# One instruction order for all engines, a narrower chunk mask and a crossbar transpose for two more pairs of heads, in an attention and feed-forward kernel

## The chip, the cores and the metric

The kernel runs on one core of a Trainium2 chip. The metric is the device time of one execution in microseconds (us), lower is better; the time before is the median of three runs. A core has five engines that each work through their own list of instructions: TensorE (PE in the profile, with its weight loads as PEld), VectorE (DVE), ScalarE (ACT), GpSimd (POOL), and SyncE (SP), which here only issues transfers. They wait for each other through semaphores. Sixteen DMA engines move data.

## The reference

The first half is causal attention over four batches of eight heads, 768 positions, head dimension 64. The keys are divided into 24 chunks of 32; each query keeps the six chunks with the highest upper bound on its score. The second half is a feed-forward block with a spatial gate.

```
k_min, k_max = min, max of k over each chunk of 32
ub     = sum_d max(q * k_min, q * k_max)             # a bound for each query and chunk
ub     = where(chunk is not later than the query's own, ub, -1e9)
top    = argsort(ub)[-6:]
scores = q @ k.T / 8, kept where the key's chunk is in top and key <= query
attn   = softmax(scores) @ v                         # -> x, (4, 768, 512)

h    = relu(x @ w_in);  u, v = h[:512], h[512:]      # per token
v_n  = (v - mean(v)) / sqrt(var(v) + 1e-6)
v_s  = w_spatial @ v_n + b_spatial                   # across the tokens
out  = (u * v_s) @ w_out
```

## The kernel before

The 32 heads are worked in 16 pairs, four pairs to a batch. A pair is first prepared: the keys are transposed on TensorE, VectorE takes the maximum and minimum of each chunk, the queries are transposed and split into a positive and a negative part, and matmuls of 48 columns (two heads of 24 chunks) form the bounds. A mask matmul opens the group and pushes later chunks down. VectorE then takes the best eight and marks the chunks below the sixth.

```python
def bounds(self):
    ub = self.ub = ps_tr.tile([P, 512], F32, tag="tr", name="ub")
    mm(ub[:, 0:(NQT - 1) * W], lhsT=sub_chunk, rhs=later, start=True, stop=False)     # L219, 240 columns
    for qi in range(1, NQT):
        for m in range(2):
            mm(ub[:, (qi - 1) * W:qi * W], lhsT=self.rq[:, m, ...], rhs=self.km[:, m]...)   # L222
```

For query tile `qi` the best eight are taken over the first `4 * (qi + 1)` chunks alone. The marks stand beside the queries in one tile `qs`; that tile, transposed, is the score operand `a`, so that one matmul adds the score and a large negative number for each chunk left out. For pairs 0 to 7 TensorE transposes it and ScalarE (for two halves VectorE) copies it out of PSUM; from pair 8 on the DMA crossbar does both.

```python
def a_transpose(self, hi):
    if self.i >= 8:
        if hi == 0:
            nc.sync.dma_start_transpose(out=self.a..., in_=self.qs...)     # L246
        return
    self.tr = self.trans_tile()
    for t in range(NQT):
        nc.tensor.transpose(self.tr[...], self.qs[:, t, 2 * hi:2 * hi + 2, :], identity)   # L251
def a_copy(self, hi):
    if self.i >= 8:
        return
    copy = nc.vector.tensor_copy if self.i < 2 and hi == 0 else nc.scalar.copy
    copy(self.a[:, :, hi, :], self.tr...)                                  # L257
```

Then each head is worked: six groups of score matmuls (L266; in the first batch with a matmul that adds the triangle, L269), each followed by an exponential on ScalarE (L271) that takes it out of one of three PSUM buffers; value matmuls (L289), and a normalisation on VectorE (L297). Later batches have the triangle set by GpSimd (L278). When a batch's four pairs are done and transposed (L310 on TensorE for the first batch and the last pair, the crossbar for the others), its feed-forward part can start: four kinds of matmul groups, v, u, s and o (all on L388), 108 matmuls of 512 columns for each batch.

The order comes from beats. Each step is registered at a beat, 12 beats to a pair; the feed-forward steps of batch `b` are spread over the 48 beats from `(b + 1) * 48 + 13`. The framework takes the steps in the order of the beats as a priority and settles each engine's order itself when the kernel is built, by durations of its own; only TensorE's steps before beat 6 are fixed as written.

```python
    first, count = (b + 1) * HP * BEATS + 13, HP * BEATS
    for cost, fn in steps:
        at(first + done * count // total, fn)
        done += cost

with tc.manual_schedule(engines={mybir.EngineType.PE}):
    for beat in sorted(b for b in beats if b < 6):
        for fn, args in beats.pop(beat):
            fn(*args)
for beat in sorted(beats):
    for fn, args in beats[beat]:
        fn(*args)
```

Of the kernel before, what the change touches and what calls it, by code (L numbers as in the profile page):

```python
# [10 lines left out]
F32 = mybir.dt.float32  # L11
# [35 lines left out]

@with_exitstack
def kernel(
# [12 lines left out]
    B, H, S, D = q.shape  # L62
# [4 lines left out]
    NQT = S // P  # L67
    NDO = DM // P
    KO = DH // P
    HP = H // 2  # L70
    NPAIR = B * HP
    CPT = P // CHUNK
    scale = 1.0 / math.sqrt(D)
    mm = nc.tensor.matmul

# [4 lines left out]
    ps_sc = ctx.enter_context(tc.psum_pool(name="ps_sc", bufs=3))  # L80
    ps_tr = ctx.enter_context(tc.psum_pool(name="ps_tr", bufs=1))
    ps_acc = ctx.enter_context(tc.psum_pool(name="ps_acc", bufs=1))
    ps_ml = ctx.enter_context(tc.psum_pool(name="ps_ml", bufs=3))

    def ml_tile():
        return ps_ml.tile([P, 512], F32, tag="mlp", name="mlp")
# [3 lines left out]

    BEATS = 12
    beats = defaultdict(list)

    def at(beat, fn, *args):
        beats[beat].append((fn, args))

    HALF = ((0, D), (D, 2 * D))


    NB = 4
    v_ring = [ring.tile([P, 4, NQT, D + 2], F16, name=f"vt{i}") for i in range(3)]
    qs_ring = [ring.tile([P, 2, NQT, 4, D], F16, name=f"qs{i}") for i in range(3)]
# [5 lines left out]
    later = cp.tile([P, (NQT - 1) * 2 * NCH], F16)  # L110
    expand = cp.tile([D, S], F16)
    eps_t = cp.tile([P, 1], F32)

    def init_identity():
        nc.vector.memset(identity, 0.0)
        nc.gpsimd.affine_select(out=identity, in_=identity, compare_op=Alu.not_equal, fill=1.0,
                                base=0, channel_multiplier=1, pattern=[[-1, P]])

    def init_ring(i):

        nc.vector.memset(qs_ring[i][:, :, :, 0:4:3, :], 0.0)

    def init_small():
        nc.vector.memset(km_ring[0], 0.0)
        nc.vector.memset(km_ring[1], 0.0)
        nc.vector.memset(eps_t, 1e-6)
        for t in v_ring:
            nc.vector.memset(t[:, :, :, D:D + 2], 1.0)

    def init_expand():  # L130

        nc.vector.tensor_scalar(expand.rearrange("d (c s) -> d c s", s=CHUNK),
                                in0=identity[0:D, 0:NCH].unsqueeze(2).to_broadcast([D, NCH, CHUNK]),
                                scalar1=NEG, scalar2=None, op0=Alu.mult)
        nc.vector.tensor_copy(sub_chunk.rearrange("d (c s) -> d c s", s=CHUNK),
                              identity[:, 0:CPT].unsqueeze(2).to_broadcast([P, CPT, CHUNK]))

    def init_masks():

        nc.gpsimd.memset(later, 0.0)  # L140
        lv = later.rearrange("p (t h c) -> p t h c", h=2, c=NCH)
        nc.gpsimd.affine_select(out=lv, in_=lv, compare_op=Alu.is_ge, fill=NEG, base=CPT,
                                channel_multiplier=1, pattern=[[CPT, NQT - 1], [0, 2], [-1, NCH]])
# [4 lines left out]
    def init_kh(i):  # L148
        for hi, (d0, d1) in enumerate(HALF):
            nc.scalar.copy(kh_ring[i][hi][d0:d1, :], expand)  # L150


    W = 2 * NCH
    xT = {}
    tiles = {}

    class Pair:
        def __init__(self, i):
            self.i = i
            self.b, self.hp = divmod(i, HP)  # L160
            self.heads = [4 * (self.hp // 2) + self.hp % 2 + 2 * hi for hi in range(2)]
            self.qs = qs_ring[i // 2 % 3][:, i % 2]
            self.kh, self.km = kh_ring[i % NB], km_ring[i % 2]
            self.e = {}

        def k_transpose(self):
            if self.i < 16:
                self.kT = kT = ps_ml.tile([P, S], F16, tag="mlp", name="kTp")
                for t in range(NQT):
                    nc.tensor.transpose(kT[:, t * P:(t + 1) * P], self.k[:, t], identity)  # L170
            else:
                self.kT = sb.tile([P, S], F16, tag="kT", name="kT", bufs=3)
                nc.sync.dma_start_transpose(out=self.kT.rearrange("d (t s) -> d t s", s=P),
                                            in_=self.k.rearrange("p t h d -> p (t h d)"))

        def k_max(self):
            self.kmm = sb.tile([P, 2, NCH], F16, tag="kmm", name="kmm")
            nc.vector.tensor_reduce(self.kmm[:, 0, :], self.kT.rearrange("d (c ch) -> d c ch", ch=CHUNK),  # L178
                                    axis=AX.X, op=Alu.max)

        def k_min(self):
            nc.vector.tensor_reduce(self.kmm[:, 1, :], self.kT.rearrange("d (c ch) -> d c ch", ch=CHUNK),  # L182
                                    axis=AX.X, op=Alu.min, negate=True)

        def k_bounds(self):
            for hi, (d0, d1) in enumerate(HALF):
                copy = nc.gpsimd.tensor_copy if 2 <= self.i < 4 else nc.scalar.copy
                s0, s1 = HALF[1 - hi]
                copy(self.km[d0:d1, :, hi], self.kmm[s0:s1])

        def k_operand(self, hi):
            d0, d1 = HALF[1 - hi]
            copy = nc.scalar.copy if self.i < 1 else nc.vector.tensor_copy
            copy(self.kh[hi][d0:d1], self.kT[d0:d1])  # L194

        def trans_tile(self):

            if self.b == 0:
                return ps_ml.tile([P, S], F16, tag="mlp", name="trm")
            return ps_tr.tile([P, S], F16, tag="tr", name="tr")  # L200

        def q_transpose(self):
            self.tr = self.trans_tile()
# [3 lines left out]
        def q_parts(self, m):  # L207
            if m == 0:
                self.rq = sb.tile([P, 2, S], F16, tag="rq", name="rq")
                nc.vector.tensor_scalar(self.rq[:, 0, P:S], in0=self.tr[:, P:S], scalar1=0.0, scalar2=None, op0=Alu.max)  # L210
            elif self.i < 1:
                nc.scalar.activation(self.rq[:, 1, P:S], self.tr[:, P:S], func=Act.Relu, scale=-1.0)
# [4 lines left out]
        def bounds(self):  # L217
            ub = self.ub = ps_tr.tile([P, 512], F32, tag="tr", name="ub")
            mm(ub[:, 0:(NQT - 1) * W], lhsT=sub_chunk, rhs=later, start=True, stop=False)  # L219
            for qi in range(1, NQT):  # L220
                for m in range(2):
                    mm(ub[:, (qi - 1) * W:qi * W], lhsT=self.rq[:, m, qi * P:(qi + 1) * P],  # L222
                       rhs=self.km[:, m].rearrange("p h c -> p (h c)"), start=False, stop=(m == 1 and qi == NQT - 1))

        def top(self, step):
            ub = self.ub
            if step == 0:
                self.max8 = sb.tile([P, NQT - 1, 2, 8], F32, tag="max8", name="max8")
            for qi in (1, 2, 3) if step == 0 else (4, 5):
                for hi in range(2):  # L230
                    c0 = (qi - 1) * W + hi * NCH
                    nc.vector.max(self.max8[:, qi - 1, hi, :], ub[:, c0:c0 + CPT * (qi + 1)])  # L232
# [7 lines left out]

        def a_transpose(self, hi):
            if hi == 0:
                self.a = sb.tile([P, NQT, 2, P], F16, tag="a", name="a")
            if self.i >= 8:
                if hi == 0:
                    nc.sync.dma_start_transpose(out=self.a.rearrange("d t h s -> d (t h) s"),  # L246
                                                in_=self.qs.rearrange("p t c d -> p (t c d)"))
                return
            self.tr = self.trans_tile()
            for t in range(NQT):  # L250
                nc.tensor.transpose(self.tr[:, t * P:(t + 1) * P], self.qs[:, t, 2 * hi:2 * hi + 2, :], identity)  # L251

        def a_copy(self, hi):
            if self.i >= 8:
                return
            copy = nc.vector.tensor_copy if self.i < 2 and hi == 0 else nc.scalar.copy
            copy(self.a[:, :, hi, :], self.tr.rearrange("d (t s) -> d t s", s=P))  # L257


        def scores(self, hi, g):  # L260
            if g == 0:
                self.e[hi] = sb.tile([P, EW], F16, tag="e", name="e", bufs=3)
            self.sc = sc = ps_sc.tile([P, 512], F32, tag="sc", name="sc")
# [6 lines left out]
            width = sum(n for (_, _, n, _) in TILES[g])  # L270
            nc.scalar.activation(out=self.e[hi][:, g * 512:g * 512 + width], in_=sc[:, 0:width], func=Act.Exp, scale=scale)  # L271

        def triangle(self, hi):
            if self.b == 0:
                return
# [5 lines left out]


        def values(self, hi, blocks, first=False, last=False):
            if first:
                av = ps_acc.tile([P, 512], F32, tag="acc", name="acc")
                self.av = av[:, 0:NQT * (D + 1)].rearrange("p (t c) -> p t c", c=D + 1)
            for n, (t, qi) in enumerate(blocks):
# [11 lines left out]

        def x_transpose(self):  # L300
            if self.hp == 0:
                xT[self.b] = ml.tile([P, NDO, S], F16, tag="xT", name="xT")
            dst = xT[self.b][:, self.hp, :]
            if 4 <= self.i < NPAIR - 1:
                nc.sync.dma_start_transpose(out=dst.rearrange("p (t s) -> p t s", s=P),
                                            in_=self.x16.rearrange("p t h d -> p (t h d)"))
            else:
                tr = self.trans_tile()
                for t in range(NQT):
                    nc.tensor.transpose(tr[:, t * P:(t + 1) * P], self.x16[:, t, :, :], identity)  # L310
                nc.vector.tensor_copy(dst, tr)

    def source(x, b, h, n):
        return x[b, h:h + n].rearrange("h (so si) d -> si (h so) d", si=P)

    def load_k(g, hi, xy=None):
        b, hp = divmod(2 * g, HP)
        if ("k", g) not in tiles:  # L320
# [274 lines left out]
```

The softmax here doesn't subtract the row's maximum and nothing guards it: scores larger than these inputs give would overflow.

## Time and profile before

| | |
|---|---|
| time | 208.62 us, median of three (208.17 to 208.92) |
| span of the profiled execution | 206.9 us |
| DMA, software queue (loads, issued by GpSimd) | 12.20 MB, 89.8% of the span on 16 engines |
| DMA, hardware queue (stores and crossbar transposes, issued by SyncE) | 14.75 MB, 36.4% |
| chain that ended last, by engine | PE 69%, ACT 17%, DVE 8%, issue 2%, DMA 2% |

An engine's share is an average over the span. The slices cut the span into 40 equal parts, and each digit is an engine's busy share in tenths. The chain follows the last instruction back, at each step to what released it. Windows give busy time in stretches of one's choice. A timeline line gives the start, the time from the first start to the last end of the merged instructions, the engine, the line of the kernel, and in brackets how long the engine was idle before and what ended that. Matmuls overlap, and their ends are modelled, so for TensorE the distance between starts tells more than the durations.

### The profile page before, as it was taken

Reading aid. Unit: us, or ns where it says so; the run is one execution under the profiler, and the core shown is the slowest. Engines: PE = TensorE matmul, PEld = TensorE weight load, DVE = VectorE, ACT = ScalarE, POOL = GpSimd, SP = SyncE. Lnnn points to the kernel's source line nnn. Section 1 sums busy time; section 2 is a strip of 40 time slices with the busy share of each in tenths; the row PEclk is TensorE's granted clock in tenths of the full one; section 3 lists DMA queues with packets and bytes.
Section 4 is the critical chain, followed back from the end, with each engine's and each line's share of the span. In section 5 each row is a group of like instructions: output and inputs, shape, how many; then the busy total and the mean of one; then the engine's idle time right before and its main releaser. Section 6 shows DMA issues by size and latency. Waiting matters only on the chain.

```text
span 206.9 us, 5068 instructions
## 1 busy us (share of the span) xinstructions
PE 187.8 (91%) x1922; PEld 115.1 (56%) x1922; DVE 154.5 (75%) x454; ACT 158.1 (76%) x326; POOL 80.5 (39%) x100
## 2 busy tenths in 40 slices
PE   0368999898899999999999999999999999999992
PEld 0266776775666665656655656565555454444440
DVE  6467979989799989899797999887647456365520
ACT  4797989899998889785989996669999830666042
POOL 7997659596992463236114111111111110000000
PEclk9999999999999999999999999999999999999999
DMA  5999999999999999979998926648782124540356
GB/s 38 92 118 154 140 178 158 173 177 167 177 162 162 97 119 128 135 130 147 149 278 153 180 62 57 127 88 158 181 166 65 38 29 92 187 152 3 72 128 256
DMA packets 114424, 27.27 MB, mean 132 GB/s; under 512 B 109536, under 2 KB 110816, under 8 KB 114400
## 3 DMA queue, kind: packets, MB, share of 16 engines
q0 software_dynamic: 76544, 12.20, 89.8%
q1 hardware_dynamic: 37856, 14.75, 36.4%
q8 instruction: 15, 0.25, 0.5%
q14 instruction: 9, 0.07, 0.1%
HBM read 24.38 MB, written 6.29 MB: 148 GB/s over the span
## 4 chain that ended last, share of the span: by engine, by line
PE 69%; ACT 17%; DVE 8%; issue 2%; DMA 2%; POOL 0%; DVEq 0%; ACTq 0%; POOLq 0%
PE mlp L388 40%; PE sc L266 12%; ACT e L271 10%; PE acc L289 7%; PE kTp L170 2%; ACT a L257 2%; DVE kmm L178 2%; PE ub L222 2%; DMA k<-in_k_dram 2%; PE trm L251 2%; ACT vraw L398 1%; PE tr L205 1%; DVE vn L412 1%; DVE kmm L182 1%; ACT u L420 1%
## 5 line engine op out<-in xcount | busy, mean ns | idle before, releaser
L271 ACT ACTIVATE e<-sc 128x512 f16<-128x512 f32 x192 | 96.9, 553 | 14.8 <-PE sc L266 13.4
L266 PE MATMUL sc<-a,kh 128*128 128x512 f16 (+3 forms) x256 | 65.5, 308 | 2.1 <-ACT e L271 1.5
L388 PE MATMUL mlp<-w_in_sb,xT 128*128 128x512 f16 x192 | 53.0, 379 | 0.1
L278 POOL TENSOR_SCALAR_AFFINE_SELECT e<-e 128x768 f16<-128x768 f16 x24 | 20.9, 869 | 66.3 <-ACT e L271 66.3
L289 PEld LDWEIGHTS <-e 128*128 128x128 f16 x672 | 31.4, 97 | 17.0 <-DVE x L297 3.8
L388 PE MATMUL mlp<-vn,wsT 128*128 128x512 f16 x144 | 37.3, 379 | 0.0
L289 PE MATMUL acc<-vt,e 128*128 128x65 f16 x672 | 35.3, 193 | 0.7 <-DVE x L297 0.4
L266 PEld LDWEIGHTS <-kh 128*128 128x128 f16 x256 | 22.7, 98 | 13.3 <-issue 0.8
L437 ACT COPY o<-mlp 128x512 f32<-128x512 f32 x24 | 14.1, 586 | 19.5 <-PE mlp L388 19.1
L400 DVE BATCH_NORM_STATS2 stats<-vraw 128x6 f32<-128x512 f32 x24 | 16.6, 693 | 12.9 <-ACT vraw L398 12.5
L388 PE MATMUL mlp<-w_out_sb,gT 128*128 128x512 f16 x96 | 25.1, 379 | 0.0
L388 PEld LDWEIGHTS <-xT 128*128 128x128 f16 x192 | 17.2, 97 | 12.6 <-issue 0.4
L427 DVE SCALAR_TENSOR_TENSOR g<-mlp,b_col,u 128x512 f16<-128x512 f32 x24 | 17.9, 748 | 7.3 <-PE mlp L388 6.2
L232 DVE MAX8 max<-ub 128x8 f32<-128x8 f32 (+4 forms) x160 | 15.6, 165 | 5.1 <-PE ub L222 4.9
L388 PEld LDWEIGHTS <-wsT 128*128 128x128 f16 x144 | 12.9, 98 | 10.4
L178 DVE TENSOR_REDUCE kmm<-kTp 128x24 f16<-128x768 f16 x16 | 15.2, 948 | 3.7 <-PE kTp L170 2.7
L297 DVE TENSOR_TENSOR x<-acc,rec 128x384 f16<-128x384 f32 x32 | 17.6, 551 | 0.4
L336 POOL DMA_DIRECT2D qs<-in_q_dram x14 | 14.6, 1049 | 5.9 <-PE sc L266 5.9
L194 DVE COPY kh<-kTp 64x768 f16<-64x768 f16 x30 | 16.5, 549 | 0.5
L398 ACT ACTIVATE vraw<-mlp 128x512 f32<-128x512 f32 x24 | 14.4, 601 | 3.0 <-PE mlp L388 3.0
L420 ACT ACTIVATE u<-mlp 128x512 f16<-128x512 f32 x24 | 14.3, 598 | 1.7 <-PE mlp L388 1.5
L327 POOL DMA_DIRECT2D k<-in_k_dram x14 | 14.4, 1045 | 2.5 <-PE kTp L170 1.8
(67 smaller groups left out, 230.2 us busy)
## 6 DMA issues: line engine op xcount, KB each, us to landing
out_dram<-o SPq DMA_DIRECT2D x24, 256.0 KB, 2.3
vt<-in_v_dram POOLq DMA_DIRECT2D x8, 384.0 KB, 8.8
k<-in_k_dram POOLq DMA_DIRECT2D x14, 192.0 KB, 8.1
qs<-in_q_dram POOLq DMA_DIRECT2D x14, 192.0 KB, 7.5
ws_raw<-in_moe_w_spatial_dram POOLq DMA_DIRECT2D x6, 192.0 KB, 6.9
w_in_sb<-in_moe_w_in_dram POOLq DMA_DIRECT2D x8, 128.0 KB, 6.9
w_out_sb<-in_moe_w_out_dram POOLq DMA_DIRECT2D x4, 128.0 KB, 7.9
k<-in_k_dram POOLq DMA_DIRECT2D x4, 96.0 KB, 3.4
```

The costliest lines, as they stand in the source:

```text
L178: nc.vector.tensor_reduce(self.kmm[:, 0, :], self.kT.rearrange("d (c ch) -> d c ch", ch=CHUNK), axis=AX.X, op=Alu.max)
L194: copy(self.kh[hi][d0:d1], self.kT[d0:d1])
L266: mm(sc[:, col:col + n], lhsT=self.kh[hi][:, t * P:(t + 1) * P], rhs=self.a[:, q0 // P:(q0 + n) // P, hi, :], start=True, stop=not diag)
L271: nc.scalar.activation(out=self.e[hi][:, g * 512:g * 512 + width], in_=sc[:, 0:width], func=Act.Exp, scale=scale)
L278: nc.gpsimd.affine_select(out=blk, in_=blk, compare_op=Alu.is_ge, fill=0.0, base=0, channel_multiplier=-1, pattern=[[0, NQT], [1, P]])
L289: mm(self.av[:, qi, :], lhsT=self.e[hi][:, c:c + P], rhs=self.v[hi][:, t, 0:D + 1], start=first and n == 0, stop=last and n == len(blocks) ...
L297: nc.vector.tensor_tensor(self.x16[:, :, hi, :], in0=self.av[:, :, 0:D], in1=rec.to_broadcast([P, NQT, D]), op=Alu.mult)
L388: mm(st[group][:, 0:cols], lhsT=lhsT, rhs=rhs, start=(j == 0), stop=(j == n - 1))
L398: nc.scalar.activation(st["vraw"][:, ti, :], h, func=Act.Relu)
L400: nc.vector.bn_stats(stats, st["vraw"][:, ti, :])
L420: nc.scalar.activation(st["u"][:, ti, :], h, func=Act.Relu)
L427: nc.vector.scalar_tensor_tensor(g, in0=vs, scalar=b_col[:, ti:ti + 1], in1=st["u"][:, ti, :], op0=Alu.add, op1=Alu.mult)
```

## The change

Three things change.

1. **Order.** The kernel now holds a small model of the core. It knows each step's engine, its duration, the latency between engines, the number of each buffer, and DMA service times, all as constants in the code. It runs a list scheduling over all steps: again and again it takes the step that can start first on any engine, and among those on one engine within 0.02 us of each other the one with the lower priority number. The priorities are the beats of before, with finer places within a pair's preparation. The steps are then emitted in that order under a manual schedule, and so every engine's order is fixed. Scores and exponentials, matmuls and evacuations, formerly one step, are now separate ones. The purpose is an order that goes by durations of this chip and not of a general model.
2. **Mask.** Since the best eight are taken over the chunks up to the query's own tile, only the four chunks of that tile need a mask: 5 tiles x 2 heads x 4 = 40 columns. The mask tile and the instructions that set it up shrink with it.
3. **Score operand.** Pairs 6 and 7 go through the crossbar too (`pa` is 6 where the old code had 8).

The plan also moves the start of a batch's feed-forward priorities from 13 to 8 beats (`mlp_first`). The other parameters stand for what the kernel before did; paths that they switch off, such as a crossbar transpose of the keys, aren't taken.

```diff
+class Sim:
+    def run(s,verbose=False):
+        ...
+        while n<N:
+            for e,c in cand.items():
+                for o in c:
+                    t=max(f,o.ready); ok=True
+                    for (p,k) in o.acq:      # buffers: wait until the old user is done
+                        ...
+                    lst.append((t,o))
+                tm=min(t for t,_ in lst)
+                t,o=min(((t,o) for t,o in lst if t<=tm+0.02),key=lambda x:(x[1].prio,x[1].idx))
+                if best is None or t<best[0]: best=(t,o)
+            ...
+            emitted.append(o); n+=1
 ...
+DEF=dict(BEATS=12,pa=8,dve_a=2,kb_pool=(2,3),xp=4,mlp_first=13,mlp_mul=1.0,sc=3,tr=1,acc=1,ml=3,kbuf=3,qbuf=3,vbuf=3,ebuf=3,late=240,chunk=2,
+  lk=40,lq=36,lv=18,kdma=99,shift=4,prep=0.0,lag=0.0,kp=27)
 ...
+                op(f'ex{i}{hi}{gg}','ACT',.493 if gg<5 else .16,.104,deps=[f'sc{i}{hi}{gg}'],...,prio=t0+6*hi+gg+.1)
 ...
+        first=(b+1)*HP*BE+p['mlp_first']; count=HP*BE*p['mlp_mul']
 ...
+PLAN = {'late': 40, 'mlp_first': 8, 'pa': 6}
 ...
-    later = cp.tile([P, (NQT - 1) * 2 * NCH], F16)
+    later = cp.tile([P, (NQT - 1) * 2 * CPT], F16)
 ...
-            mm(ub[:, 0:(NQT - 1) * W], lhsT=sub_chunk, rhs=later, start=True, stop=False)
+            own = bass.AP(ub.tensor, ub.offset + CPT, [list(ub.ap[0]), [W + CPT, NQT - 1], [NCH, 2], [1, CPT]])
+            mm(own, lhsT=sub_chunk, rhs=later, start=True, stop=False, skip_group_check=True)
 ...
+    order = build(PLAN)
+    order.run()
 ...
-    with tc.manual_schedule(engines={mybir.EngineType.PE}):
-        for beat in sorted(b for b in beats if b < 6):
-            ...
-    for beat in sorted(beats):
-        for fn, args in beats[beat]:
-            fn(*args)
+    with tc.manual_schedule():
+        for o in order.emitted:
+            acts[o.name]()
```

## The prediction

> **What bounds the kernel now.** I read the engine shares and the slices first, then the chain of work that ended last, then windows of 8 us, and last the timelines of TensorE and ScalarE in the stretch that the windows pointed at.
>
> ```profile
> PE 187.8 (91%) x1922; PEld 115.1 (56%) x1922; DVE 154.5 (75%) x454; ACT 158.1 (76%) x326; POOL 80.5 (39%) x100
> ...
> PE   0368999898899999999999999999999999999992
> ACT  4797989899998889785989996669999830666042
> ```
>
> TensorE looks full from the fifth slice on. But matmul ends are modelled and overlap, so I rebuilt its true load: instructions that start in each window, times the spacing at which the timeline shows them following each other undisturbed. The chain ends with 146 matmuls of 512 columns in 31.53 us, so 216 ns each; six transposes take 0.33 us; a value matmul of 65 columns 31 ns (21 in 0.65 us); a bound matmul of 48 columns 26 ns (below); one head's eight score matmuls have 2688 columns, so 1.14 us. The window from 24 to 32 us, for example, has 18 score matmuls (2.57), 13 of the triangle (0.74), 42 values (1.30), 35 transposes (2.00), 11 bounds and one mask (0.38): 7.0 us of work, where the busy column says 7.70.
>
> ```profile
> 8.00:16.00 8.00, 5.17 (x44) 4.01 (x45) 4.79 (x17) 7.15 (x11) 8.00 (x9) 1.00 1.70 109
> 16.00:24.00 8.00, 7.02 (x89) 4.97 (x87) 6.60 (x22) 6.73 (x16) 5.25 (x8) 1.00 3.10 151
> 24.00:32.00 8.00, 7.70 (x120) 6.04 (x119) 6.55 (x23) 7.09 (x16) 5.42 (x9) 1.00 2.26 166
> 32.00:40.00 8.00, 7.24 (x118) 5.53 (x118) 7.92 (x32) 7.08 (x16) 6.64 (x11) 1.00 2.22 165
> 40.00:48.00 8.00, 7.09 (x110) 5.47 (x109) 7.01 (x20) 7.78 (x18) 7.15 (x9) 1.00 1.70 171
> 48.00:56.00 8.00, 6.76 (x92) 4.61 (x91) 6.90 (x21) 7.48 (x17) 6.13 (x8) 1.00 1.92 175
> ...
> 80.00:88.00 8.00, 8.00 (x92) 5.12 (x91) 7.22 (x25) 6.44 (x15) 1.55 (x2) 1.00 2.01 134
> ```
>
> Columns: window, its length, then busy time and count for PE, PEld, DVE, ACT and POOL, then clock, DMA share and GB/s. The same reckoning gives 5.8, 7.0, 6.4, 6.4 and 6.1 us of TensorE work in the five windows from 16 to 56 us: 31.8 of 40, so 8.2 us idle, most of it hidden in the busy column. From 56 to 80 us it gives 7.8, 7.9 and 7.4; from 80 us to the last matmul at 203 us 8.0 and more in every window (an instruction at an edge is counted whole). So there are two kernels in one. **Until 55 us**, when the first matmul of the feed-forward part starts (55.09 us in the timeline), there is only attention of the first batch, fed by a chain of latencies up to 15 us and by ScalarE after that (36.2 of the 40 us from 16 to 56). **From then on** TensorE has more ready work than it can do; time goes down there only by taking work off it. The last 35 us are feed-forward matmuls alone, back to back.
>
> **What the Trainium skill says.** "Perfetto Trace Analysis", section Identifying the Most-Contended Engine, holds that matmul busy share is no good measure of how near TensorE is to its limit; the window above, 7.70 busy for 7.0 of work, agrees. "TensorE: Matmul & The Clock Gate", section Back-to-back issue gap, gives columns over 2.4 plus 2.5 ns, which is 216 ns for 512 columns, and a floor near 25 ns for few columns; 216 and 26 ns here agree. (The 131 ns for 512 columns that the same section names as sustained is not what this trace shows.) "PSUM — Partial Sum Buffer", section The four PSUM rules, says that a group's first matmul clears the written marks of the whole bank, and that a later matmul overwrites where the mark is clear; that is why 40 mask columns can stand for 240 with nothing put in the place of the rest. No time hangs on it. "DMA: Bandwidth & Descriptors", section Issuing engines are not separate DMA queues, says that transfers from all issuers run on the same 16 engines; the trace agrees in that the crossbar transposes of the score operand land after 3.7 to 8.4 us.
>
> **The change, part by part.**
>
> Mask. The mask matmul shrinks from 240 to 40 columns.
>
> ```profile
> 63.80 0.26 PE L219 MATMUL ub<-later,sub_chunk 128*128 128x240 f16 x1
> 63.90 0.41 PE L222 MATMUL ub<-km,rq 128*128 128x48 f16 x10
> 64.16 0.27 PE L368 MATMUL wtr<-identity,ws_raw 128*128 128x128 f16 x2
> ```
>
> The starts are what counts: 0.10 us for the mask, 0.26 for ten bounds. A mask of 40 columns should cost what a bound does, 0.026, so 0.074 is saved each time. Ten of the sixteen (pairs 6 to 15) lie in the full stage: **0.7 us**. The other six fall into a stretch that TensorE doesn't bound. On GpSimd the mask's two set-up instructions (0.36 and 0.48 us before) shrink, which moves later loads forward a little; I count nothing for it.
>
> Score operand. Pairs 6 and 7 give up 2x2x6 transposes on TensorE and four copies on ScalarE.
>
> ```profile
> 68.48 0.50 PE L251 MATMUL tr<-identity,qs 128*128 128x128 f16 x6
> 68.81 0.59 PE L388 MATMUL mlp<-w_in_sb,xT 128*128 128x512 f16 x2
> ...
> 69.09 0.81 ACT L257 COPY a<-tr 128x768 f16<-128x768 f16 x1
> ```
>
> Start to start six take 0.33 us; four times that is **1.3 us** in the full stage. The four copies (59.6, 63.0, 69.1 and 73.8 us in the timeline; 0.7 us of ScalarE's time each) are 2.8 us off ScalarE between 59 and 75 us, where TensorE still lacks 0.2, 0.1 and 0.6 us to be full and once waits 0.28 us for such a copy. I give **0.5** for that. In exchange there are two more crossbar transposes. The bounds of pair 6 are selected at about 58.7 us and its first scores come at about 66: some 7 us for a transfer whose median is 4.7 and whose worst 8.4. Hidden in most cases.
>
> Order. The gaps that a better order can close are those of ScalarE between 16 and 56 us, since it feeds that stage. The timeline's bracketed idle times there are 0.30, 0.77, 0.26, 0.32, 0.58, 0.19, 0.35, 0.23 and 0.44: 3.4 us. The largest:
>
> ```profile
> 18.61 3.21 ACT L271 ACTIVATE e<-sc 128x512 f16<-128x512 f32 x7 [0.77 <-PE sc L266]
> ...
> 28.53 0.80 ACT L257 COPY a<-trm 128x768 f16<-128x768 f16 x1 [0.32 <-PE trm L251]
> 29.91 0.80 ACT L257 COPY a<-trm 128x768 f16<-128x768 f16 x1 [0.58 <-PE trm L251]
> ```
>
> The last two show the kind: the third pair's selection is done at 26.2 us on VectorE, but its transposes start only at 28.0 and 29.4, because TensorE's fixed order has put them behind scores and values that wait for ScalarE. A list that sets such short pieces by durations taken from the chip should put them first. I choose seven tenths of the 3.4, **2.4 us**. Everything after 55 us then moves forward with it. The choice is mine: some of the gaps hang on the chain (bounds, best six, selection, transpose, copy), which no order shortens.
>
> Feed-forward priority. It starts 5 of a pair's 12 beats sooner in the list. It can't start before the first batch's last transpose, and after that TensorE is full either way: 0. At the end it leaves fewer such matmuls for the stretch behind the last attention. Before, some 152 followed it, 44 of them belonging to the third batch; five beats are 108 x 5/48, or 11 matmuls. 33 remain to cover the last pair's normalisation, so no new hole.
>
> Start and tail. The first loads, the first pair's chain (TensorE's first matmul at 5.75 us, first exponential at 15.3) and the last copy and store (203.05 to 206.9) are the same operations; I allow 0.3 us either way.
>
> Sum: 0.7 + 1.3 + 0.5 + 2.4 = 4.9, say 5.0 with the smaller mask set-up; 208.6 - 5.0 = **203.6 us**.
>
> **Rivals.** *Only the removed work counts.* The order before was fixed at build time too, by a scheduler with durations of its own, and the first 55 us may hang on the chain of latencies and on VectorE (7.92 of 8 from 32 to 40 us) and not on order. Then 2.0 us are left: 206.6. For it speaks that ScalarE is already 90% busy there; against it the 1.8 us for which finished selections wait.
>
> *The fixed order meets a late transfer.* All engines now run one list in order. Where a load or crossbar transpose lands later than the list assumed (loads of keys land after 6.1 to 10.5 us, and the DMA is full until about 98 us), an engine stops with ready work behind it, and the feed-forward matmuls can't fill in. Two or three such stops of 1 to 2 us eat the gain: 207 to 210. Against it: loads are issued far ahead (the last keys at 77 us), and the queue of ready feed-forward work was as fixed before.
>
> *Order wins more than the gaps.* If the first pair's chain also gets shorter (the first scores wait 0.5 us behind another pair's transposes at 13.1 to 14.4 us) and nearly all of the 3.4 is closed: 201 or somewhat less.
>
> **Range and chances.** Removed work is nearly certain, 1.7 to 2.5 us. The order is worth between -1.5 and +5. That gives 200.4 to 207.2 for eight in ten. Faster by over 2% means under 204.45: the centre is 0.85 us below it, with a spread of some 3 us, hence 0.57; within 2% 0.36; slower 0.07.
>
> **What would show it.** Right: transposes of the score operand on TensorE 72 and no longer 96, crossbar transposes of it 10 and no longer 8; the first feed-forward matmul at about 52.5 us in place of 55.1; ScalarE's idle time between 16 us and that point near 1 us; a gapless TensorE from there to the end; the stretch from the first feed-forward matmul to the last 2 to 2.5 us shorter. Wrong: a start of the feed-forward part at 55 us (then the first rival), or waits of over 0.5 us on TensorE behind a DMA or a score operand after 55 us (then the second); a hole of TensorE between the last attention and the last batch's feed-forward part would show that the earlier priority was not free.

## The result and the profile after

The changed kernel takes 216.0 us, against 208.8 for the kernel before beside it: a ratio of 1.033 (95% interval 1.0285 to 1.0376). The 216.0 is the median of three runs; a fourth, at 219.3, was in a slower state of the chip, and with it the median is 216.3, from which the expectations below count. The kernel was to be faster by 5 us and is slower by some 7.

First the engine shares and two engines' slices from the page of the changed kernel, then its windows (columns as before: window, length, busy time and count of PE, PEld, DVE, ACT, POOL, then clock, DMA share, GB/s).

```profile
PE 187.9 (87%) x1898; PEld 113.4 (53%) x1898; DVE 156.7 (73%) x454; ACT 153.8 (72%) x322; POOL 80.5 (37%) x100
...
PE   0449979898998896996999998999999999999982
ACT  6585977999988656374889796668999950565033
```

```profile
8.00:16.00 8.00, 3.82 (x39) 3.03 (x40) 6.05 (x19) 6.16 (x11) 8.00 (x9) 1.00 1.74 111
...
64.00:72.00 8.00, 6.42 (x82) 4.11 (x79) 7.49 (x16) 7.38 (x20) 4.75 (x7) 1.00 2.30 139
...
80.00:88.00 8.00, 6.13 (x67) 3.56 (x66) 5.94 (x21) 4.48 (x10) 5.74 (x6) 0.88 2.47 150
...
96.00:104.00 8.00, 6.01 (x69) 3.54 (x68) 5.11 (x19) 4.19 (x8) 3.84 (x4) 1.00 1.84 149
```

Two of these windows in the kernel before (the ones from 8 and from 80 us stand in the prediction):

```profile
64.00:72.00 8.00, 7.85 (x95) 5.20 (x93) 7.61 (x28) 6.74 (x16) 2.57 (x3) 1.00 1.61 119
96.00:104.00 8.00, 8.00 (x86) 4.77 (x85) 6.79 (x19) 7.24 (x17) 1.72 (x2) 1.00 1.95 158
```

Busy PE is the same 187.9 us, with 24 matmuls fewer; what has changed is where it is not busy. Three dents are new (64, 80 and 96 us), all in the stretch that was full before, and the one from 8 us, which was there already, is deeper. To see them without the modelled ends I took every matmul's start in the trace and called lost what lies between it and the next start beyond its own spacing (columns over 2.4 plus 2.5 ns, at least 25 ns: the spacing of the prediction; differences under 10 ns are left out). Matmuls that follow each other more slowly because the granted clock is lower count as lost too. That splits each kernel's time:

| kernel | time us | first exponential at | first feed-forward matmul at | TensorE work | lost before that matmul | lost after it |
|---|---|---|---|---|---|---|
| before | 208.8 | 15.3 | 55.1 | 176.8 | 16.9 | 2.6 |
| changed | 216.0 | 17.1 | 55.6 | 174.2 | 18.1 | 11.7 |

Work fell by 2.6 us, as reckoned (1.3 each for mask and transposes). Lost time before the feed-forward part rose by 1.2, and after its start by 9.1. The chain of work that ended last shows the dents at 80 and 96 us; the one at 64 us has another cause and comes further down (start us, us, what):

```profile
67.11 13.27 DMA a<-qs
...
80.93 0.43 POOL qs L425
...
83.97 0.90 POOL e L594
...
89.86 8.77 DMA gT<-g
98.75 0.75 DVE g L716
99.64 0.57 DVE x L613
100.26 0.45 PE acc L605 x9
```

A crossbar transpose of the score operand (pair 7) is under way for 13.3 us. GpSimd's next query load must not overwrite `qs` before it has been read; the triangle (L594) stands behind that load in GpSimd's order, and value matmuls wait for the triangle. The dent at 96 us hangs on a second crossbar transpose: `gT<-g`, a piece of the gate's result, lands after 8.8 us, VectorE's next gate step waits for it, the normalisation of `x` behind that step comes late, and value matmuls wait for the normalisation. The waits between 80 and 104 us say the same (who waits for whom: total us, times, longest):

```profile
ACT e L588 <- PE sc L579: 9.2, 10, 2.9
...
POOL qs L425 <- DMA a<-qs: 6.0, 1, 6.0
...
PE acc L605 <- POOL e L594: 1.9, 1, 1.9
```

The list had planned with other landing times: by its own constants the operand's transposes of pairs 6 and 7 land 5.4 us after their issue. They took 7.8 and 13.3.

Of what the changed parts do by themselves, the mask is as expected (0.03 us from its start to the bounds' start, 0.10 before), and the transposes on TensorE are 72.

```profile
61.37 0.18 PE L536 MATMUL ub<-later,sub_chunk 128*128 128x40 f16 x1
61.40 0.41 PE L539 MATMUL ub<-km,rq 128*128 128x48 f16 x10
```

The first exponential comes 1.85 us late. ScalarE's and VectorE's timelines of the first pair show how:

```profile
7.83 0.79 ACT L515 COPY kh<-kTp 64x768 f16<-64x768 f16 x1 [1.12 <-DVE kmm L506]
9.65 0.79 ACT L515 COPY kh<-kTp 64x768 f16<-64x768 f16 x1 [1.02 <-DVE kmm L506]
...
17.14 1.13 ACT L588 ACTIVATE e<-sc 128x512 f16<-128x512 f32 x2 [1.83 <-PE sc L582]
```

```profile
8.66 0.96 DVE L506 TENSOR_REDUCE kmm<-kTp 128x24 f16<-128x768 f16 x1 [0.86 <-ACT kh L515]
...
12.18 0.56 DVE L549 MAX8 max<-ub 128x8 f32<-128x8 f32 x6 [0.76 <-PE ub L539]
12.66 0.94 DVE L506 TENSOR_REDUCE kmm<-kTp 128x24 f16<-128x768 f16 x1
13.52 0.44 DVE L549 MAX8 max<-ub 128x8 f32<-128x20 f32 x4
13.99 0.56 DVE L515 COPY kh<-kTp 64x768 f16<-64x768 f16 x1
14.59 0.41 DVE L554 TENSOR_TENSOR qs<-ub,max 128x240 f16<-128x240 f32 x1
```

Two things are to be seen. Maximum, copy, minimum and copy of the same transposed keys take turns on the two engines, three of the four with about a microsecond of idle time in brackets: both engines read one PSUM tile, and the instruction list has each of the four wait for the one before. The list's model knows nothing of that; it lets both read at once. And between the first pair's two halves of the best eight and its selection the list has put pieces of the second pair (0.94 and 0.56 us). In the model a VectorE step's result is ready 0.08 us after the engine is free again; another step that can start at once is "first", since only differences under 0.02 us are settled by priority. So a pause of 0.08 us draws a step of 0.9 into the chain that everything waits for.

### The profile page after: what moved, and what is told of

Its sections match the earlier page's. It is cut to its first block, busy times and chain, and to the rows that moved or that the text cites. A ratio compares the mean times of both kernels' runs of the same rounds, so it can differ in the third digit from the quotient of the medians.

```text
span 214.9 us, 5013 instructions
## 1 busy us (share of the span) xinstructions
PE 187.9 (87%) x1898; PEld 113.4 (53%) x1898; DVE 156.7 (73%) x454; ACT 153.8 (72%) x322; POOL 80.5 (37%) x100
## 2 busy tenths in 40 slices
DMA packets 117560, 28.06 MB, mean 131 GB/s; under 512 B 112672, under 2 KB 113952, under 8 KB 117536
## 4 chain that ended last, share of the span: by engine, by line
PE 55%; DVE 21%; DMA 13%; ACT 3%; issue 2%; POOL 2%; POOLq 0%; DVEq 0%
PE mlp L676 34%; PE sc L579 9%; DVE kmm L506 7%; DMA a<-qs 6%; PE acc L605 6%; DMA gT<-g 6%; DVE kh L515 3%; DVE x L613 3%; DVE max L549 2%; PE ub L539 2%; DMA k<-in_k_dram 2%; PE kTp L490 1%; PE tra L566 1%; DVE rq L528 1%; DVE g L716 1%
## 5 line engine op out<-in xcount | busy, mean ns | idle before, releaser
L588 ACT ACTIVATE e<-sc 128x512 f16<-128x512 f32 x192 | 95.1, 556 | 21.9 <-PE sc L579 18.9
L676 PE MATMUL mlp<-w_in_sb,xT 128*128 128x512 f16 x192 | 52.7, 379 | 0.1
L594 POOL TENSOR_SCALAR_AFFINE_SELECT e<-e 128x768 f16<-128x768 f16 x24 | 21.0, 874 | 71.6 <-ACT e L588 71.6
L605 PE MATMUL acc<-vt,e 128*128 128x65 f16 x672 | 36.3, 194 | 4.9 <-DVE x L613 2.8
L676 PE MATMUL mlp<-vn,wsT 128*128 128x512 f16 x144 | 40.3, 389 | 0.0
L506 DVE TENSOR_REDUCE kmm<-kTp 128x24 f16<-128x768 f16 x32 | 29.6, 948 | 7.6 <-PE kTp L490 6.8
L716 DVE SCALAR_TENSOR_TENSOR g<-mlp,b_col,u 128x512 f16<-128x512 f32 x24 | 18.0, 749 | 16.5 <-PE mlp L676 13.3
L676 PE MATMUL mlp<-w_out_sb,gT 128*128 128x512 f16 x96 | 26.9, 379 | 0.6 <-DVE g L716 0.6
L676 PEld LDWEIGHTS <-xT 128*128 128x128 f16 x192 | 17.6, 97 | 14.9 <-issue 0.7
L425 POOL DMA_DIRECT2D qs<-in_q_dram x14 | 14.5, 1050 | 9.3 <-DMA a<-qs 6.0
L549 DVE MAX8 max<-ub 128x8 f32<-128x8 f32 (+4 forms) x160 | 15.3, 165 | 1.3 <-PE ub L539 1.1
```

The costliest lines, as they stand in the source:

```text
L425: nc.gpsimd.dma_start(out=t.rearrange("p x t d -> p (x t) d"), in_=source(q, b, h, 2))
L506: nc.vector.tensor_reduce(self.kmm[:, m, :], src, axis=AX.X, op=op, negate=(m == 1))
L549: nc.vector.max(self.max8[:, qi - 1, hi, :], self.ub[:, c0:c0 + CPT * (qi + 1)])
L594: nc.gpsimd.affine_select(out=blk, in_=blk, compare_op=Alu.is_ge, fill=0.0, base=0, channel_multiplier=-1, pattern=[[0, NQT], [1, P]])
L605: mm(self.av[:, qi, :], lhsT=self.e[hi][:, c:c + P], rhs=self.v[hi][:, t, 0:D + 1], start=first and n == 0, stop=last and n == len(blocks) ...
L676: mm(st[kind, ti], lhsT=lhsT, rhs=rhs, start=(j == 0), stop=(j == n - 1))
```

## The experiments

**The parts undone.** Three runs of the changed kernel with its plan edited, and one of the kernel before with the crossbar alone.

```diff
-PLAN = {'late': 40, 'mlp_first': 8, 'pa': 6}
+PLAN = {'late': 40, 'mlp_first': 8, 'pa': 8}      # operand back
+PLAN = {'late': 40, 'mlp_first': 13, 'pa': 6}     # priority back
+PLAN = {'late': 40, 'mlp_first': 13, 'pa': 8}     # order and mask only
```
```diff
-            if self.i >= 8:      # the kernel before, in a_transpose and a_copy
+            if self.i >= 6:
```

> The changed kernel with the crossbar for the score operand from pair 8 on again (pa 8); order by the list, mask and early feed-forward priority stay. Theory (crossbar in the full stretch): the two added transposes land late among the loads, and what waits for them costs some 6 us between 64 and 104 us; undone, the time is 209 to 211, no transpose of the operand takes over 9 us, and GpSimd's 6.0 us wait for one is gone. Rival (the list's order is worse by itself): at least 214.

> The changed kernel with the feed-forward priority at 13 beats again; the crossbar for pairs 6 and 7 stays. Theory (crossbar in the full stretch): 215 to 217, as changed. Rival (the early priority draws gate transposes into the full stretch and holds attention back): 211 to 213.

> Only the list's order and the narrow mask: pa 8 and priority at 13. Theory: within 1 us of the run with the operand alone undone, 209 to 211; the first exponential stays near 17.1 us, since that delay belongs to the order. Rival (order): 214 or more. Rival (priority): clearly under the run with the operand alone undone.

> The kernel before with one part of the change: crossbar for the score operand from pair 6 on. If the late transposes hurt whatever the order, 211 to 214. If they hurt only because a fixed list puts loads and triangles behind them, 206 to 208.5, by 1.3 us of transposes less on TensorE.

Measured: operand back 211.8 us (ratio 1.0157, 1.0136 to 1.0177); priority back 217.7 (1.042, 1.0398 to 1.0442); order and mask only 215.4 (1.0331, 1.0309 to 1.0352); crossbar from pair 6 in the old kernel 219.2 (1.0514, 1.0482 to 1.0546). Operand back and priority back are a little above what their theories gave (209 to 211 and 215 to 217), and with the operand back the transpose of pair 10 still took 10.1 us; for order and mask only, the rival (at least 214) came true; the crossbar in the old kernel cost more than either theory had.

With the list the crossbar accounts for 4.1 us (216.0 against 211.8): from 80 to 104 us 5.3 us more are lost than with the operand back, and 1.3 us of transposes are saved. In the framework's order the same edit costs 10.5. There the order itself moved too from the edited pair on, so not all of that is the transfer's; but 7.7 us are TensorE's own waits for the operand in two pieces, and in the window of the longer one the granted clock is 0.68. TensorE's timeline of that run, and that window:

```profile
70.02 0.61 PE L266 MATMUL sc<-a,kh 128*128 128x512 f16 x1 [6.29 <-DMA a<-qs]
```
```profile
64.00:72.00 8.00, 1.98 (x10) 1.16 (x11) 1.32 (x4) 1.43 (x4) 0.86 (x1) 0.68 1.70 127
```

So the harm does not need the list. The rival theories each hold a part: operand back stays 3.1 us above the kernel before, and order and mask alone 6.7, so the order costs something by itself; and I had the early priority down as worth nothing, but a list made without it takes 3.6 us more (215.4 against 211.8).

**Why the transposes are late.** A fourth query buffer takes away GpSimd's wait; leaving loads out empties the DMA as well.

```diff
-    for i in range(3): op(f'ring{i}','DVE',.63,...)      # and the two conditions g<3
+    for i in range(4): op(f'ring{i}','DVE',.63,...)      # and g<4
-PLAN = {'late': 40, 'mlp_first': 8, 'pa': 6}
+PLAN = {'late': 40, 'mlp_first': 8, 'pa': 6, 'qbuf': 4}
```
```diff
     def load_q(g, hi, xy=None):        # the second run, on top of the first
+        if g in (4, 5):
+            return
     def load_v(g):
+        if g in (3, 4, 5):
+            return
```

> The changed kernel with four query buffers in place of three, so that GpSimd's load of the next queries no longer waits until a late crossbar transpose has read the old ones; crossbar from pair 6 on stays. Theory A (loads and triangles stuck behind that wait are the loss): GpSimd's 6.0 us wait is gone and the time is 211.5 to 213. Theory B (the late operand itself holds the scores): 215 to 217, the two transposes still landing after 9 to 13 us.

> As the run with four query buffers, but the query loads of pairs 8 to 11 and the value loads of pairs 6 to 11 are left out (old contents are used in their place), which empties the DMA between about 50 and 95 us. If full DMA engines make the transposes late, those of pairs 6 and 7 land within 6 us and the time is 208.5 to 211.5. If they are late for another reason (their own queue, the wait for the selection), they stay above 9 us and the time is that of the run with four buffers.

Measured: four buffers 216.2 us (1.036, 1.0339 to 1.038), fewer loads 211.4 (1.0138, 1.0115 to 1.0161). With four buffers nothing is won: GpSimd's 6.0 us wait is gone, and TensorE waits 3.3 us for `a` itself. The chain through the query load that the profile after shows is thus one way in which a late transpose reached TensorE, not the cause. With fewer loads TensorE, VectorE and ScalarE work in the very same order as with four buffers, TensorE no longer waits for `a`, and the time is that of the operand undone. Not all of the 4.8 us gained need be the operand's: leaving loads out can spare other waits too. Issues of the operand's transposes between 65 and 69 us (pair 7; the last number is us from issue to landing), with four buffers and then with fewer loads:

```profile
a<-qs SPq DMA_TRANSPOSE x1, 13.0
```

```profile
a<-qs SPq DMA_TRANSPOSE x1, 4.2
```

The same instruction, at the same place in the same list, lands after 13.0 us among the loads and after 4.2 without many of them; in the 5 us from 66 us on the packets of the loads take 156% of the 16 engines' time in the first run (several are under way at once) and 64% in the second. Pair 6's takes 8.0 against 7.8 us, so that the expectation of under 6 missed there; two key loads, issued at 57.1 us, stay beside it. This bears out what "DMA: Bandwidth & Descriptors" of the Trainium skill says in its section Issuing engines are not separate DMA queues: transfers that SyncE and GpSimd issue run on the same 16 engines, so that this transpose shares them with the loads.

**The first chain.** Dependencies in the list alone, on top of operand back:

```diff
-deps=[f'kT{i}'],acq=[('kmm',i)]                    # kmax
+deps=[f'kT{i}']+(['sel0'] if i==1 else []),acq=[('kmm',i)]
-deps=[f'kT{i}'],acq=[('kh',i)]                     # the key operand's two copies
+deps=[f'kT{i}']+([['kmin0'],['rq01']][hi] if i==0 else ['sel0'] if i==1 else []),acq=[('kh',i)]
# kmin1 after kmax1, rq01 after kb0, the set-up copies of kh2 and kh3 after kop01
```

> The list's order with the operand undone (pa 8), and dependencies added to the list alone, so that the first pair's chain isn't interrupted: VectorE does the first pair's best eight and selection before the second pair's maxima, ScalarE copies the key operand after both maxima. Theory (the delay of the first exponential from 15.3 to 17.1 us is worth its length, since the stage behind it is a chain): first exponential near 15.3 us and 210.0, 1.8 under the run with the operand alone undone (211.8). Rival (until 56 us ScalarE and VectorE are full anyway, and the chain's delay was made up): first exponential earlier, time unchanged within 0.6.

Measured: 210.2 us (1.0079, 1.0055 to 1.0103), 1.65 less than without. VectorE's line shows the best eight in one piece again, and the first exponential comes at 15.09.

```profile
11.48 0.91 DVE L549 MAX8 max<-ub 128x8 f32<-128x8 f32 x10 [2.33 <-PE ub L539]
12.42 0.41 DVE L554 TENSOR_TENSOR qs<-ub,max 128x240 f16<-128x240 f32 x1
```

The delay (2.0 us by the two first exponentials) was worth most of its length, as the theory had it; the first feed-forward matmul moved from 55.0 to 53.2.

**The framework's order.** Two single parts in the kernel before: the mask as in the diff of the change, and the priority.

```diff
-        first, count = (b + 1) * HP * BEATS + 13, HP * BEATS
+        first, count = (b + 1) * HP * BEATS + 8, HP * BEATS
```

> The kernel before with one part of the change: the mask of 40 columns. By the sum of the prediction 0.7 us in the full stretch: 207.8 to 208.2 against 208.7. The framework's order may also move with it, which could hide so small a gain: then 208 to 210.

> The kernel before with one number changed: the feed-forward steps spread from beat 8 of a batch and no longer 13. If the earlier priority is of use by itself, under 208.0; if it only repairs what the list's order spoils, 208 to 209.5; if the framework's order simply moves, anything up to 212 with most of the difference before the first feed-forward matmul.

Measured: mask 211.7 us (1.0148, 1.0128 to 1.0168), priority 213.9 (1.0234, 1.0176 to 1.0292). Both are slower than expected, and neither prices its part, since both edits moved the framework's order of all engines. With the mask the first feed-forward matmul stands at 57.9 us in place of 55.1, and from there to the end it is 151.7 us against 151.8. By these two runs the order of the kernel before is one that a small edit leaves, and for a worse one.

**The hole from 64 to 72 us.** It is in the changed kernel and in all list runs so far (2.4 to 2.9 us lost). In the list of the run with the first chain protected no feed-forward matmul starts for 8 us there. The three PSUM buffers for transposes and feed-forward groups are given out in turn. One holds a pair's transposed keys (`kTp`), the next two a piece each of the transposed spatial weight (`wtr`), and then it is the keys' buffer's turn again: the next group (`mlp`) must wait until VectorE has read the keys for the last time. TensorE's timeline of that run, and VectorE's copies from `wtr` and last copy from `kTp`:

```profile
62.45 0.60 PE L676 MATMUL mlp<-w_in_sb,xT 128*128 128x512 f16 x2
...
63.10 0.50 PE L490 MATMUL kTp<-identity,k 128*128 128x128 f16 x6
63.44 0.50 PE L461 MATMUL wtr<-identity,ws_raw 128*128 128x128 f16 x6
...
63.97 0.49 PE L461 MATMUL wtr<-identity,ws_raw 128*128 128x128 f16 x6
...
71.04 0.59 PE L676 MATMUL mlp<-w_in_sb,xT 128*128 128x512 f16 x2
```
```profile
64.70 0.99 DVE L463 COPY wsT<-wtr 128x768 f16<-128x768 f16 x2
...
70.55 0.54 DVE L515 COPY kh<-kTp 64x768 f16<-64x768 f16 x1
```

Four edits of the list, on top of the protected first chain; the second includes the first, and the third and the fourth each include these two:

```diff
-prio=pr((3 if hi==0 else 8))                        # second copy of the key operand
+prio=pr((3 if hi==0 else 3.2 if i>1 else 8))        # key buffer freed early
-deps=[f'wsp{j}' for j in range(NQT)]+['id1']
+deps=[f'wsp{j}' for j in range(NQT)]+['id1']+([f'wsc{so-1}',f'u0{so-1}.2'] if so else ['v05.2'])   # spacing
```
```diff
-PLAN = {'late': 40, 'mlp_first': 8, 'pa': 8}
+PLAN = {'late': 40, 'mlp_first': 8, 'pa': 8, 'prep': 3}            # preparation later (only in its own run)
-deps=lk+['id1']                                                    # key transposes
+deps=lk+['id1']+([f'sc{i-2}05'] if i>=8 else [])                   # held (without prep)
```

> The run with the first chain protected (210.2), and in the list the second copy of the key operand right behind the first, so that the PSUM buffer with the transposed keys is given back about 4 beats sooner. Theory (after the first feed-forward matmul the list has holes where the three PSUM buffers for transposes and feed-forward groups are all held by pieces that wait for VectorE): the stretch from the first feed-forward matmul to the end shortens from 155.1 to 153 to 154, time about 209. Rival (the holes come from single late instructions, 0.5 us each, of VectorE): unchanged within 0.6.

> As the run before it, and the six transposes of the spatial weight no longer run in a bunch: each waits for the copy of the one before and for a feed-forward group. Theory: TensorE's hole between 64 and 71 us closes, another 1.5 us: 207.5. Rival: unchanged within 0.6.

> As the run before it, with each pair's preparation 3 beats later in the list (its model's best by 1.2 us, in a small scan). If the list's model is good enough to choose by, 206 to 207; if its choices don't carry to the chip, at or above the run before it.

> The run with buffers and spacing (209.7), and from pair 8 on the key transpose is held in the list until the last scores of the first head two pairs before. Theory (the list starts a pair's keys as soon as it can, and then a PSUM buffer of the three is held for 6 us by pieces that VectorE takes late, so that no feed-forward group can start): TensorE's loss between 64 and 72 us falls from 2.3 to under 1, its loss after the first feed-forward matmul from 5.9 to about 4, time 207.5 to 208.5. Rival (ScalarE or VectorE is full there, and the loss moves elsewhere): 209 to 210 with the loss in another window.

Measured: 209.5 us (1.0042, 1.0024 to 1.0059), 209.7 (1.0031, 1.002 to 1.0042), 211.1 (1.01, 1.006 to 1.0141) and 208.6 (1.0, 0.999 to 1.0011). The first two brought the start of the feed-forward part forward, to 51.9 and 51.7 us, but the stretch behind it grew no shorter (155.1, then 156.1 and 155.7 us) and the hole stayed (2.7 and 2.3 us lost), so the bunched weight transposes weren't it, and both theories missed. The list's best choice by its own model by 1.2 us came out 1.4 slower. Holding back the keys closed the hole, 2.3 to 0.5 us lost; about half of the gain was lost again in the next window (0.0 to 1.0), and the 208.6 is just above the theory's 207.5 to 208.5. So what blocks the buffers there is a pair's keys, transposed as soon as they can be and read late by VectorE. "Perfetto Trace Analysis", section Optimization Strategy, of the Trainium skill says of gaps that repeat for a stretch on the engine that should be saturated that they can mean "there isn't enough SBUF/PSUM for the next tile to be allocated". Here it is a single hole with that cause, and three buffers were enough once none was taken early. This list is level with the kernel before.

**The crossbar moved once more, and the mask priced in a fixed order.** All three from the run with the key transposes held: the crossbar from pair 10 (`'pa': 10`), the crossbar from pair 6 (`'pa': 6`), and the mask of 240 columns under the plan for 40. The first two make a new list; the third keeps every engine's order and changes the mask's own instructions alone.

> As the run before it, with the score operand through the crossbar only from pair 10 on. Its transposes cost TensorE 0.33 us for each of four halves, 1.3 us. If the crossbar still holds something up between 75 and 100 us, where the DMA is full in all runs, the time is at or under the run before it; if not, 1.0 to 1.5 us above it.

> The run with the key transposes held (208.6), with the crossbar from pair 6 on again. If the two transposes in the full stretch cost time in any order (4.5 us in the changed kernel's list, 10.5 in the framework's), 212 to 216, with TensorE losing 4 us or more between 64 and 104 us. If a list without holes can bear them, 207.5 to 209.

> The run with the key transposes held (208.6) in the very same order on every engine, but with the mask of 240 columns. This prices the mask without moving anything else. By the sum of the prediction ten masks of 0.074 us lie where TensorE is full: 0.5 to 0.9 above that run, 209.3. If the mask hides behind other waits, within 0.3.

Measured: crossbar from 10, 213.3 us (1.0219, 1.0204 to 1.0233); from 6, 217.2 (1.041, 1.0384 to 1.0437); wide mask 208.8 (1.0001, 0.9989 to 1.0014). The crossbar from 10 fits neither of its two answers: 4.7 us more, where the added transposes are 1.3. TensorE waits 3.0 us, to 102.1 us, for the crossbar's transpose of `x`, issued at 93.4 and landed after 8.7 us. From 6, TensorE waits for the operand in one piece, and the granted clock of the windows from 64 and 72 us is 0.75 and 0.82:

```profile
72.13 1.04 PE L579 MATMUL sc<-a,kh 128*128 128x512 f16 x2 [6.39 <-DMA a<-qs]
```

The wide mask can't be told from the narrow one.

The split of the main runs, as in the first table:

| kernel | time us | first exponential at | first feed-forward matmul at | TensorE work | lost before | lost after |
|---|---|---|---|---|---|---|
| operand back | 211.8 | 17.1 | 55.0 | 175.6 | 17.4 | 6.1 |
| first chain protected | 210.2 | 15.1 | 53.2 | 175.6 | 15.6 | 6.0 |
| buffers and spacing | 209.7 | 15.1 | 51.7 | 175.6 | 14.8 | 5.9 |
| key transposes held | 208.6 | 14.9 | 51.9 | 175.6 | 15.0 | 5.3 |
| the same, wide mask | 208.8 | 15.4 | 52.0 | 176.8 | 14.5 | 4.1 |
| the same, crossbar from 6 | 217.2 | 15.1 | 52.7 | 174.2 | 15.7 | 13.4 |

## Why the prediction was wrong

**Where it failed.** The step that failed first is "Score operand ... Hidden in most cases". The 1.3 us of TensorE work went, but the term had the wrong sign: 4.1 us lost in the changed kernel, 8.6 in the repaired list, 10.5 in the old kernel (the last two with moved orders and a lower clock in them). I had set a median of 4.7 us, taken over pairs 8 to 15, against some 7 us of room. Six of those eight were issued after 99 us. In the stretch where pairs 6 and 7 fall the DMA digits of the page stand at 9, and there the operand's transpose took 7.8 to 13.3 in all runs with the full loads but once (4.1, for pair 7 in the old kernel, issued at 73.4 us, after TensorE had stood still). I had also reckoned for pair 6 alone: in the changed kernel its transpose just fits (7.8), and pair 7's takes the 13.3. The case to set against 7 was that of the first such transposes, pair 8's 8.4, which already exceeded the room. And the kernel before has another crossbar transpose in that very stretch, that of `x` at 60.9 us, of half the size, which took 8.8 us to land:

```profile
xT<-x SPq DMA_TRANSPOSE x1, 8.8
```

**The second step** was "after that TensorE is full either way". It was nearly true of the order before (2.6 us lost; the prediction's 8.0 and more in every window from 80 us is 7.3 from 160 to 168 when each matmul is counted once, by its start) and is not a property of the stage. In the list 6.1 us are lost after the feed-forward part starts even without the crossbar, 2.9 of them in the hole that the key buffers cause. From this false step also came "0" for the priority: in the list it was worth 3.6 us with the crossbar undone (215.4 to 211.8) and 1.7 with it (217.7 to 216.0). How it fills holes is not shown.

**The third** was "first pair's chain ... the same operations; I allow 0.3 us". The operations were the same, the order was not: 1.85 us. With the chain protected the run gained 1.65.

**Order, 2.4 us.** The mechanism was there, hidden by the chain. ScalarE's bracketed idle times between 16 us and the first feed-forward matmul, 3.4 us before, add up to 5.5 in the changed kernel (1.8 of it just before the first exponential). With the chain protected they are 2.7, and with the key buffer freed and the spacing 1.7; I had said near 1. In that last run 14.8 us are lost on TensorE before the feed-forward part in place of 16.9, and that part starts at 51.7 us; I had said about 52.5. The gain of 2.1 is near the 2.4, but the list gives it back later (5.9 lost against 2.6), so that nothing is left at the end.

**Mask, 0.7 us.** Sized too high. In one and the same order the two ratios to the kernel before, 1.0000 and 1.0001, have intervals of 0.001 each way, so the difference is some 0.4 us at most. TensorE's work does fall by 1.2 us, and its lost time is 1.7 higher in those two profiles: what the mask gave up became waiting. What is waited for there is not shown.

**ScalarE's relief, 0.5 us.** Nothing of it is to be seen; ScalarE's slices between 70 and 102 us stand at 3 to 7 tenths, where they stood at 5 to 9, and between 80 and 104 us it waits 9.2 us for scores.

**Rivals.** The first rival's sign, a feed-forward part that starts at 55 us, came true (55.6), but not for its reason: the broken first chain ate what the order could gain. The second rival, a late transfer that meets a fixed order, named the right transfer and had it too small (207 to 210). The list is not what makes it dangerous: in the framework's order the same transfer stops TensorE for 6.3 us in one piece.

## What to carry to other kernels

A transfer's landing time has to be read in the stretch where the new one will run; a median over a whole kernel mixes a full DMA with an empty one, here 13.0 and 4.2 us for the same instruction in the same place. A stage that is full in one order isn't full in every order: look at who holds its buffers before counting a gain further up as a gain at the end. A list scheduler that takes whatever can start first puts long steps into short pauses of the critical chain, and takes scarce buffers early; give its model the waits that the trace shows (engines taking turns at one PSUM tile, late landings; no run here tried such a model), and price small edits in an order that doesn't move with them.

## What the runs showed of the hardware that was not expected

- ScalarE and VectorE took turns at one PSUM tile of transposed keys, 0.8 to 1.1 us idle each time; the waits are set in the program, and no run here leaves them out.
- Two more crossbar transposes of the operand raise the moved data from 27.27 to 28.06 MB and the packets from 114424 to 117560; the packets are few (3%), the delays large.
- TensorE's granted clock is below 1.00 in windows of some runs. In the changed kernel it is 0.88 and 0.91 in the windows from 80 and 88 us, in the dents there, and 1.00 in the kernel before. In the two runs with a wait of 6.3 or 6.4 us for the operand it is 0.68 and 0.75 in the window from 64 us, and 0.90 and 0.82 in the next. So a part of what the tables call lost in these runs is a slower clock and not waiting. Lost time alone does not tell where the clock falls: with four query buffers 5.0 us are lost between 88 and 104 us, and the clock stays at 1.00.
